# A one-core attention and gated-MLP kernel: a new order of all its operations, with other banks and other shares of work

## The chip, the cores and the metric

The kernel runs on one core of one Trainium2 chip. A core has five engines with one instruction stream each, which meet only through semaphores: PE (TensorE: matrix products into PSUM, with the weight loads as a stream of their own, PEld), DVE (VectorE), ACT (ScalarE), POOL (GpSimd) and SP (SyncE, which here only asks for transfers). Transfers are moved by 16 DMA engines; SP, ACT and POOL can ask for them. The metric is device microseconds of one execution.

## The reference, cut to what matters

Linear attention with decay, in blocks of 64 positions (4 batches, 8 heads, 768 positions, 64 channels), and on its output a gated MLP with a product over positions:

```python
for b in range(nb):                       # 12 blocks of 64
    intra = (qb @ kb.T) * Dmask           # Dmask[i,j] = lam**(i-j) for i >= j, else 0
    out[block] = intra @ vb + (qb * lam**(pos+1)) @ kv_state
    kv_state = lam**64 * kv_state + (kb * lam**(63-pos)).T @ vb
x = out, heads side by side               # 4 x 768 x 512
h = relu(x @ w_in); u, v = halves of h    # 512 each
v_n = (v - mean(v)) / sqrt(var(v) + 1e-6)
v_s = w_spatial @ v_n + b_spatial         # over the 768 positions of a batch
result = (u * v_s) @ w_out                # 4 x 768 x 512, float32
```

## The kernel before, in words

The decay is split: k is multiplied by a power of lam that falls with the position and q by its inverse, so the mask is only 0 or 1. Positions are taken in 12 steps of 256, three to a batch (step n is in batch n // 3); a step has two halves c of 128 positions.

One string, `ORDER`, names every operation in the order in which the program issues it, as `name.arguments.engine` with the engine as the last letter (T for PE, D for DVE, A for ACT, P for POOL, S for SP). A loop at the end (lines 538 to 541) calls the function for each; nothing else decides about order. Each engine runs its own operations in the order of the string; semaphores are put in where one needs another's result or a buffer or bank that is still read. The last one or two numbers of most PE operations and of their evictions are PSUM banks (0 to 6; bank 7 holds the running state).

```python
with tc.manual_schedule():
    for token in ORDER.split():
        name, *args, e = token.split(".")
        ops[name](e, *map(int, args))
```

By step n, attention:

- `LQ`, `LK`, `LV` ask for q, k, v of a step (512 KB each; line 192, SP; three buffers each). `HL.1.3` is a write of one element by POOL into the buffer that q of step 3 will use, so that this load waits for it (line 264). `GT.1.1` and `GN.2.1` are copies of one element on POOL that make it wait for the load of q of step 1 and for an operation of batch 0 (lines 239 and 464).
- `QM`, `KM` multiply halves of q and k by the decay into bfloat16 (line 289, on POOL or DVE). In steps 0 to 4 PE transposes them (`TQ`, `TK`, line 319) and ACT or DVE copies the result out (`EQ`, `EK`); from step 5 on SP asks for transposes by DMA (`DQ`, `DK`, lines 306 and 302). `VC` casts v to bfloat16 (lines 177, 179 or 181, by engine).
- `SC` makes scores (line 349), `MK` masks them on DVE (line 354), `KV` adds to the running state (line 366), `SS` copies the state out, `AV` makes the attention's output (lines 387 and 396, in two parts; `FN` is a copy of one element that stands between them), `EX` copies it out as xT.

The MLP: `PV` (line 421) and `EV` give v, `BN` its statistics, `RA`, `RD`, `RB` the reciprocal deviation and the scaled mean (lines 441, 446, 451), `VN` normalises. `RB` is needed only where ACT normalises (line 457); DVE does it from mean and deviation (line 460). `PU` (line 472) and `EU` give u. `WT` and `EW` transpose w_spatial once (line 484). For each batch `GP` copies the bias into a bank, `PW` (line 498) adds the product over positions, `GM` (line 504) multiplies with u, `PO` (line 509) is the last product, `EO` evicts and `ST` stores (line 532); the last tile goes in two halves (`PH`, `EH`, `SH`).

Constants and weights: `lam` and `BR` are asked for from ACT's queue (lines 196 and 255; 32 bytes and the bias row of 3 KB); `LB`, `LN`, `LL`, `LX` make the decay tables; `BB` spreads the bias row over all partitions by a matmul with ones (line 258, PE) and `BE` copies it out. `WI.0` asks for the half of w_in that `PV` reads, `WI.1` for the half that `PU` reads, `WS` for halves of w_spatial, `WO` for w_out: all from POOL, since they are cast on the way (lines 243, 248, 252). `tab.1` loads ACT's second table. `FL` are matmuls of ones that nobody reads (line 272).

The bias row's way, as the code has it:

```python
def b_r(e):
    {"S": nc.sync, "A": nc.scalar}[e].dma_start(out=brow, in_=moe_b_spatial.unsqueeze(0))

def b_b(e, i, b):
    nc.tensor.matmul(out=bank(b)[:, 0:HW], lhsT=one_row, rhs=brow[:, i * HW:(i + 1) * HW], start=True, stop=True)
```

Of the kernel before, what the change touches and what calls it, by code (L numbers as in the profile page):

```python
# [20 lines left out]
SC.0.1.3.4.T LK.2.S EK.1.0.0.A QM.1.1.P MK.0.0.5.6.D FL.6.256.2.0.T TQ.1.0.2.T TQ.1.1.0.T EQ.1.0.2.A EQ.1.1.0.A
LV.2.S EK.1.1.1.D VC.0.P MK.0.1.3.4.D BB.1.2.T BE.1.2.A FL.1.256.1.0.T SC.1.0.0.1.T SC.1.1.5.6.T KV.0.0.T
QM.2.1.P MK.1.0.0.1.D MK.1.1.5.6.D WI.1.P AV.0.0.2.3.T FN.0.2.3.A SS.0.0.A VC.1.A BB.0.4.T WS.0.P KV.0.1.T
AV.0.1.2.3.T BE.0.4.A TQ.2.1.0.T QM.2.0.P SS.0.1.D KM.2.1.P EX.0.1.3.A EX.0.0.2.D KV.1.0.T AV.1.0.1.6.T
# [7 lines left out]
PU.0.0.5.T EU.0.0.5.A RA.2.A PU.2.0.3.T WT.2.1.1.T EW.2.1.1.D GP.0.0.0.4.A PU.2.1.0.T EU.2.0.3.A WT.1.1.2.T
WT.0.1.6.T RD.2.D VN.2.0.D VN.2.1.D LV.4.S LQ.5.S LK.5.S EU.2.1.0.A GN.2.1.P KM.3.1.P KM.3.0.P PW.0.0.0.4.T
EW.0.1.6.D EW.1.1.2.D GP.0.2.0.5.A GP.0.3.1.3.A TQ.3.2.6.T PW.0.2.0.5.T TK.3.2.1.T GM.0.0.0.4.D EK.3.2.1.D
EQ.3.2.6.A PW.0.3.1.3.T GP.0.1.0.0.A VC.3.P KM.4.0.P GM.0.2.0.5.D SC.3.0.5.6.T SC.3.1.1.2.T GM.0.3.1.3.D
GP.0.3.0.4.A QM.4.0.P QM.4.1.P KV.3.0.T MK.3.0.5.6.D LV.5.S MK.3.1.1.2.D PW.0.3.0.4.T GM.0.3.0.4.D SS.3.0.D
# [535 lines left out]
```

## Time and profile before

| | |
|---|---|
| median of 3 runs | 144.38 us (143.93 to 144.56) |
| the profiled execution | 143.63 us, span 141.9 us |
| PE busy | 132.8 us (94%) |
| DVE, ACT, POOL busy | 110.6, 76.2, 53.5 us |
| 16 DMA engines | 31.88 MB moved, 225 GB/s on average |
| product over positions (`PW`, line 498) | 192 matmuls of 384 columns |
| granted clock of PE | 1.00 throughout |

The span is the profiler's, from the first instruction to the last; the time of the same execution is 1.73 us longer. Busy time of PE counts each matmul from its start to its modelled end, and matmuls overlap, so a busy PE may still be slower than its own pace; what counts is whether it stands idle and who let it go on. Idle time of another engine costs nothing by itself.

### The profile page before, as it was taken

How to read it: one execution, taken by the hardware profiler on the slowest of the kernel's cores; microseconds unless marked ns; L12 is line 12 of the kernel's file. 1: busy time of each engine (PE TensorE's matmuls, PEld its weight loads, DVE VectorE, ACT ScalarE, POOL GpSimd, SP SyncE). 2: the span in 40 equal slices, each digit the busy share in tenths (PEclk: the TensorE clock that was granted, in tenths of full speed). 3: DMA queues.
4: the chain of work that ended last, by engine and by line, in shares of the span. 5: the costliest groups of instructions: out<-in, count | busy, mean ns of one | idle time of the engine just before them, and what ended most of it. 6: DMA issues, size and time to landing. Idle time of an engine off the chain costs nothing.

```text
span 141.9 us, 4688 instructions
## 1 busy us (share of the span) xinstructions
PE 132.8 (94%) x1980; PEld 86.7 (61%) x1997; DVE 110.6 (78%) x220; ACT 76.2 (54%) x153; POOL 53.5 (38%) x62
## 2 busy tenths in 40 slices
PE   5979979999999999999999999999999999999990
PEld 3855656768577564676566465685665655855550
DVE  3486957998696986697899789977897989984940
ACT  3136748778527666669524647697236642570041
POOL 5567973015997532196715025603700000000000
PEclk9999999999999999999999999999999999999999
DMA  3999999999999999999999899999979242310075
GB/s 84 345 346 345 230 252 210 225 337 257 334 328 239 125 236 343 306 139 347 227 260 158 209 360 241 262 329 165 291 117 259 93 170 98 128 74 0 33 294 191
DMA packets 58232, 31.88 MB, mean 225 GB/s; under 512 B 15843, under 2 KB 55267, under 8 KB 58212
## 3 DMA queue, kind: packets, MB, share of 16 engines
q1 hardware_dynamic: 55824, 28.84, 78.1%
q0 software_dynamic: 2384, 2.75, 11.4%
q8 instruction: 15, 0.25, 0.7%
q14 instruction: 5, 0.04, 0.1%
q10 hardware_dynamic: 4, 0.00, 0.0%
HBM read 24.38 MB, written 6.29 MB: 216 GB/s over the span
## 4 chain that ended last, share of the span: by engine, by line
PE 72%; DMA 14%; DVE 4%; SPq 3%; ACT 2%; issue 1%; POOL 0%; DVEq 0%; ACTq 0%
PE ps L498 21%; PE ps L472 13%; PE ps L509 13%; PE ps L421 13%; DMA win_sb<-in_moe_w_in_dram 7%; DMA q_in<-in_q_dram 4%; DMA v_in<-in_v_dram 3%; PE ps L349 3%; PE ps L396 3%; PE ps L366 3%; DVE a_sb L354 2%; SPq L192 2%; PE ps L319 2%; PE ps L387 1%; SPq L302 1%
## 5 line engine op out<-in xcount | busy, mean ns | idle before, releaser
L498 PE MATMUL ps<-wt_sb,vn 128*128 128x384 bf16 x192 | 34.0, 326 | 0.0
L354 DVE TENSOR_TENSOR a_sb<-ps,m 128x1024 bf16<-128x1024 f32 x24 | 28.6, 1216 | 2.5 <-PE ps L349 1.9
L289 POOL TENSOR_TENSOR kc<-k_in,lv 128x512 bf16<-128x512 f32 x18 | 19.2, 1080 | 22.4 <-DMA k_in<-in_k_dram 6.3
L498 PEld LDWEIGHTS <-vn 128*128 128x128 bf16 x192 | 18.1, 98 | 12.2 <-ACT vn L457 0.4
L289 POOL TENSOR_TENSOR qc<-q_in,lqn 128x512 bf16<-128x512 f32 x19 | 20.0, 1069 | 14.2 <-DMA q_in<-in_q_dram 8.5
L472 PE MATMUL ps<-xT,win_sb 128*128 128x256 bf16 x192 | 23.2, 273 | 0.0
L421 PE MATMUL ps<-win_sb,xT 128*128 128x512 bf16 x89 | 21.8, 379 | 1.2 <-DMA win_sb<-in_moe_w_in_dram 0.6
L509 PE MATMUL ps<-wout_sb,gT 128*128 128x512 bf16 x82 | 21.1, 379 | 1.0 <-issue 0.6
L504 DVE TENSOR_TENSOR gT<-ps,uT 128x384 bf16<-128x384 f32 x32 | 16.8, 551 | 6.0 <-PE ps L498 5.3
L472 PEld LDWEIGHTS <-win_sb 128*128 128x128 bf16 x192 | 18.2, 98 | 3.6
L436 DVE BATCH_NORM_STATS2 st<-vh 128x6 f32<-128x512 bf16 x24 | 16.3, 679 | 0.8 <-ACT vh L426 0.5
L426 ACT ACTIVATE vh<-ps 128x512 bf16<-128x512 f32 x20 | 11.9, 595 | 9.3 <-PE ps L421 9.3
L177 ACT ACTIVATE o_sb<-ps 128x512 f32<-128x512 f32 (+1 forms) x17 | 9.6, 567 | 12.2 <-DVE o_sb L179 8.9
L421 PEld LDWEIGHTS <-xT 128*128 128x128 bf16 x96 | 9.1, 98 | 10.6 <-DVE xT L179 0.7
L509 PEld LDWEIGHTS <-gT 128*128 128x128 bf16 x92 | 8.5, 98 | 9.1 <-DVE gT L504 0.2
L177 ACT ACTIVATE ps<-bsp 128x384 f32<-128x384 f32 x21 | 9.9, 487 | 4.6 <-DVE a_sb L354 3.8
L177 ACT ACTIVATE xT<-ps 128x512 bf16<-128x512 f32 x16 | 9.1, 595 | 4.9 <-PE ps L396 4.9
L181 POOL CAST vb<-v_in 128x1024 bf16<-128x1024 f32 x7 | 7.8, 1118 | 8.1 <-issue 5.3
L396 PE MATMUL ps<-a_sb,vb 64*64 64x128 bf16 x384 | 10.6, 217 | 0.0
L366 PEld LDWEIGHTS <-kc 64*64 64x64 bf16 x320 | 6.8, 109 | 4.9 <-issue 3.8
L426 ACT ACTIVATE uT<-ps 128x512 bf16<-128x512 f32 x16 | 9.2, 586 | 0.4 <-PE ps L472 0.4
L366 PE MATMUL ps<-vb,kc 64*64 64x64 bf16 x320 | 8.6, 194 | 0.4 <-DVE s_sb L179 0.3
(70 smaller groups left out, 167.1 us busy)
## 6 DMA issues: line engine op xcount, KB each, us to landing
q_in<-in_q_dram SPq DMA_DIRECT2D x12, 512.0 KB, 6.6
k_in<-in_k_dram SPq DMA_DIRECT2D x12, 512.0 KB, 6.3
v_in<-in_v_dram SPq DMA_DIRECT2D x12, 512.0 KB, 6.2
out_dram<-o_sb SPq DMA_DIRECT2D x23, 256.0 KB, 2.3
wsp_raw<-in_moe_w_spatial_dram POOLq DMA_DIRECT2D x2, 576.0 KB, 10.2
win_sb<-in_moe_w_in_dram POOLq DMA_DIRECT2D x2, 512.0 KB, 8.9
wout_sb<-in_moe_w_out_dram POOLq DMA_DIRECT2D x1, 512.0 KB, 7.7
out_dram<-o_sb SPq DMA_DIRECT2D x2, 128.0 KB, 1.9
```

Source lines behind the costliest of these rows:

```text
L177: nc.scalar.activation(out=o, in_=i, func=AF.Copy)
L289: vec(e).tensor_tensor(out=dst[n % NCA][:, u].rearrange("p u m o d -> p o (u m) d"), in0=src[n % NIN].rearrange("p (o u) m d -> p o u m d" ...
L354: nc.vector.tensor_tensor(out=a_sb[n % NA][:, i].rearrange("p o w j x -> p o w (j x)"), in0=ps[:, b0:b1 + 1:b1 - b0].rearrange("p o (w y) ...
L366: nc.tensor.matmul(out=pkv[row(o), u], lhsT=kc[n % NCA][row(c), u, m, o, :], rhs=vb[n % NCA][row(c), 4 * o + u, m, :], start=new and u == ...
L396: nc.tensor.matmul(out=po[c ^ o][row(w), c, i], lhsT=vb[n % NCA][row(c), 4 * o + u, j, :], rhs=a[row(c), i, o, w, j, :], start=(r == 0 and ...
L421: nc.tensor.matmul(out=bank(b), lhsT=x[:, slot(c, g)], rhs=win_sb[:, g, DH:DFF], start=(g == 0), stop=(g == NCH - 1))
L426: nc.scalar.activation(out=o, in_=i, func=AF.Relu)
L436: nc.vector.bn_stats(out=st6[p2][:, t], in_=vh[p2][:, t])
L472: nc.tensor.matmul(out=pu[:, f2].rearrange("p (c x) -> p c x", c=2), lhsT=win_sb[:, g, f * P:(f + 1) * P], rhs=x[:, slot(0, g):slot(1, g) ...
L498: nc.tensor.matmul(out=bank(b)[:, 0:HW], lhsT=vn[bb % 2][:, s, f * P:(f + 1) * P], rhs=wt_sb[:, s, i * HW:(i + 1) * HW], start=False, stop ...
L504: nc.vector.tensor_tensor(out=gT[bb % 2][:, f, cols], in0=bank(b)[:, 0:HW], in1=uT[bb % 2][:, f, cols], op=ALU.mult)
L509: nc.tensor.matmul(out=bank(b), lhsT=gT[bb % 2][:, f, t * P:(t + 1) * P], rhs=wout_sb[:, f, :], start=(f == 0), stop=(f == NCH - 1))
```

## The change

All that differs is the string `ORDER`. It names the same operations on the same data, in another order on every engine, with other PSUM banks, and gives about a hundred of them to another engine. Line numbers stay. What differs in number: `FL` matmuls (47 in before, 44 in after) and `RB` (9 and 12: after has it for the steps 0 to 2 too, some of whose `VN` are now on ACT).

Evictions and small work by engine (before, then after):

| | ACT | DVE | POOL |
|---|---|---|---|
| `GP` bias into a bank | 21, 26 | 11, 6 | |
| `EX` xT | 16, 18 | 8, 6 | |
| `EU` u | 16, 18 | 8, 6 | |
| `EV` v | 20, 18 | 4, 6 | |
| `EQ` / `EK` transposes | 7, 4 / 4, 6 | 1, 4 / 4, 2 | |
| `SS` state | 13, 10 | 7, 10 | |
| `VN` | 10, 9 | 14, 15 | |
| `VC` cast of v | 3, 5 | 2, 1 | 7, 6 |
| `EO` / `EH` outputs | 15, 14 / 2, 0 | 8, 9 / 0, 2 | |

The requests of weights keep their places among POOL's products: `WI.0` comes behind the load of q of step 1 (in before by `GT.1.1`, in after by `QM.1.1`), `WI.1` and `WS.0` behind q's product of step 2, `WS.1` behind k's product of step 2 and beside `HL.1.3`. `BR` was the second operation of ACT and comes now behind `EK.0.0`. `BB.0`, `BB.1` stand ahead of `KV.0.0` on PE; in before `BB.1` stood ahead of `SC.1` and `BB.0` behind `AV.0.0`. The cast `VC.0` goes from POOL to ACT. On POOL a half of q's product of step 8 (`QM.8.1`) now comes ahead of those of step 7, and on SP `LK.6` comes behind the transposes of step 5.

The diff, cut to the start, the stretch with `QM.8.1`, and the end; each line is a line of the string:

```diff
--- before
+++ after
@@ ORDER @@
-msk.P one.D idn.P FL.6.256.3.1.T LQ.0.S lam.A BR.A tab.0.A row.D LK.0.S FL.2.256.2.1.T LK.1.S LB.6.T LQ.1.S
-FL.16.128.0.1.T LV.0.S LV.1.S FL.6.256.2.0.T posk.P mkc.D LN.6.A LL.D LX.A QM.0.1.D QM.0.0.P KM.0.0.P KM.0.1.D
-TQ.0.0.3.T TQ.0.1.5.T EQ.0.0.3.D TK.0.0.4.T EQ.0.1.5.A EK.0.0.4.A KM.1.0.D TK.0.1.0.T FL.4.256.1.1.T
-FL.5.256.1.0.T KM.1.1.D EK.0.1.0.D GT.1.1.P LQ.2.S WI.0.P QM.1.0.D TK.1.1.1.T SC.0.0.5.6.T TK.1.0.0.T
-SC.0.1.3.4.T LK.2.S EK.1.0.0.A QM.1.1.P MK.0.0.5.6.D FL.6.256.2.0.T TQ.1.0.2.T TQ.1.1.0.T EQ.1.0.2.A EQ.1.1.0.A
-LV.2.S EK.1.1.1.D VC.0.P MK.0.1.3.4.D BB.1.2.T BE.1.2.A FL.1.256.1.0.T SC.1.0.0.1.T SC.1.1.5.6.T KV.0.0.T
-QM.2.1.P MK.1.0.0.1.D MK.1.1.5.6.D WI.1.P AV.0.0.2.3.T FN.0.2.3.A SS.0.0.A VC.1.A BB.0.4.T WS.0.P KV.0.1.T
-AV.0.1.2.3.T BE.0.4.A TQ.2.1.0.T QM.2.0.P SS.0.1.D KM.2.1.P EX.0.1.3.A EX.0.0.2.D KV.1.0.T AV.1.0.1.6.T
-FN.1.1.6.D TQ.2.0.4.T SS.1.0.A AV.1.1.1.6.T KV.1.1.T SS.1.1.D EX.1.0.1.D eps.D EX.1.1.6.A EQ.2.1.0.A EQ.2.0.4.A
-KM.2.0.P PV.0.0.5.T EV.0.0.5.D PV.0.1.2.T EV.0.1.2.A PV.1.0.6.T BN.0.0.D BN.0.1.D TK.2.1.1.T EK.2.1.1.A
-TK.2.0.3.T EK.2.0.3.D EV.1.0.6.A PV.1.1.2.T SC.2.1.0.1.T SC.2.0.4.5.T MK.2.1.0.1.D EV.1.1.2.A tab.1.A
-MK.2.0.4.5.D RA.0.A WS.1.P HL.1.3.P LQ.3.S LK.3.S LV.3.S VC.2.P PU.1.0.3.T PU.1.1.6.T EU.1.0.3.A EU.1.1.6.A
...
-LK.8.S EX.5.0.1.D EX.5.1.6.A QM.7.1.P QM.7.0.P LV.7.S PV.5.1.6.T PV.5.0.4.T PO.0.0.5.T EV.5.1.6.A EO.0.4.2.D
-BN.4.1.D PU.5.1.6.T PU.3.1.1.T GP.1.2.1.3.D LK.9.S DQ.6.S BN.4.0.D RA.4.A BN.5.1.D EU.4.1.0.D EV.5.0.4.A
-GP.1.0.1.2.A VN.3.0.A EU.3.1.1.A EO.0.0.5.A RD.4.D RB.4.D SS.6.1.D BN.5.0.D KM.8.1.P VC.7.P DQ.7.S GP.1.2.0.5.A
-RA.5.A RD.5.D VN.4.1.D RB.5.D QM.8.0.P PU.4.0.0.T EU.4.0.0.A QM.8.1.P VN.5.1.D VN.4.0.A PO.0.1.4.T PU.5.0.1.T
...
-EO.3.2.5.D PO.3.4.2.T EO.3.4.2.A ST.3.2.S ST.3.4.S PO.3.1.3.T PO.3.3.6.T EO.3.1.3.D ST.3.1.S PH.3.5.0.3.T
-EO.3.3.6.A PH.3.5.1.5.T ST.3.3.S EH.3.5.0.3.A SH.3.5.0.S FL.1.256.0.0.T EH.3.5.1.5.A SH.3.5.1.S
+lam.A LQ.0.S posk.P row.D one.D msk.P tab.0.A LK.0.S FL.1.256.0.1.T FL.6.256.1.1.T LK.1.S idn.P LB.4.T LQ.1.S
+LN.4.A LL.D mkc.D LX.A QM.0.1.P LV.0.S QM.0.0.D FL.5.256.1.0.T FL.16.128.2.1.T KM.0.1.D LV.1.S TQ.0.1.1.T
+KM.0.0.D TK.0.1.3.T EQ.0.1.1.A TQ.0.0.5.T EK.0.1.3.A KM.1.0.P KM.1.1.D LQ.2.S TK.0.0.1.T SC.0.1.3.4.T EK.0.0.1.A
+EQ.0.0.5.D eps.D FL.8.256.0.0.T MK.0.1.3.4.D BR.A QM.1.1.P LK.2.S TK.1.1.6.T SC.0.0.1.2.T QM.1.0.D EK.1.1.6.A
+FL.3.256.5.0.T WI.0.P TQ.1.1.6.T LV.2.S TK.1.0.3.T EQ.1.1.6.D MK.0.0.1.2.D TQ.1.0.4.T EK.1.0.3.A BB.0.0.T
+EQ.1.0.4.A BE.0.0.A VC.1.P VC.0.A BB.1.2.T BE.1.2.A KV.0.0.T QM.2.1.P QM.2.0.P SS.0.0.D AV.0.0.4.5.T
+SC.1.0.0.1.T SC.1.1.2.3.T KV.0.1.T tab.1.A MK.1.1.2.3.D FL.5.256.6.0.T FN.0.4.5.A SS.0.1.A KV.1.0.T WI.1.P
+MK.1.0.0.1.D TQ.2.0.2.T AV.0.1.4.5.T WS.0.P EQ.2.0.2.A AV.1.0.3.6.T EX.0.1.5.D SS.1.0.A KV.1.1.T FN.1.3.6.D
+EX.0.0.4.D KM.2.0.P TQ.2.1.5.T AV.1.1.3.6.T SS.1.1.D KM.2.1.D EX.1.1.6.A PV.0.0.2.T EX.1.0.3.A TK.2.0.1.T
+EV.0.0.2.D PV.1.1.6.T VC.2.P EQ.2.1.5.D EK.2.0.1.D PV.0.1.3.T EV.1.1.6.A BN.0.0.D HL.1.3.P WS.1.P LQ.3.S
+SC.2.0.1.2.T TK.2.1.5.T EV.0.1.3.A LK.3.S GT.1.1.P PV.1.0.0.T EK.2.1.5.A MK.2.0.1.2.D LV.3.S SC.2.1.4.5.T
+KV.2.0.T MK.2.1.4.5.D PU.0.1.6.T AV.2.0.1.3.T BN.0.1.D PU.1.1.2.T EV.1.0.0.A LQ.4.S SS.2.0.D FN.2.1.3.A
...
+EX.5.0.0.D GN.2.1.P QM.6.1.P EU.4.1.1.A PU.4.0.2.T PV.5.0.3.T EO.0.0.5.A RA.4.A PV.5.1.4.T RD.4.D EV.5.0.3.A
+EU.4.0.2.A RB.3.D VN.3.0.D BN.5.0.D PU.5.0.0.T EV.5.1.4.A LQ.7.S DQ.6.S KM.7.0.P GP.1.1.1.1.A PU.3.1.2.T
+PU.5.1.3.T BN.5.1.D GP.1.2.1.6.A KM.7.1.P EU.5.0.0.D RA.5.A PO.0.1.4.T RD.5.D RB.4.D VN.4.1.D RB.5.D SS.6.1.A
+DK.7.S LQ.9.S VN.3.1.D VN.4.0.A EU.5.1.3.D VN.5.0.D PO.0.3.0.T VN.5.1.A EU.3.1.2.A EO.0.1.4.D LV.8.S LK.9.S
+GP.1.2.0.4.A GP.1.0.1.5.A PW.1.2.1.6.T PW.1.1.1.1.T GP.1.3.1.2.A VC.7.A QM.8.1.P QM.7.1.P QM.7.0.P PW.1.2.0.4.T
+PW.1.0.1.5.T GM.1.2.1.6.D EO.0.3.0.A GP.1.0.0.6.D GM.1.2.0.4.D GM.1.1.1.1.D DQ.7.S SC.6.1.3.4.T GM.1.0.1.5.D
...
+PO.3.1.1.T ST.3.2.S ST.3.0.S GM.3.3.1.3.D PO.3.4.3.T EO.3.1.1.D PO.3.3.4.T ST.3.1.S EO.3.4.3.A ST.3.4.S
+PH.3.5.1.1.T EO.3.3.4.A EH.3.5.1.1.D ST.3.3.S SH.3.5.1.S PH.3.5.0.5.T EH.3.5.0.5.D SH.3.5.0.S
```

More of the change, by code (lines that the diff above doesn't have):

```diff
@@ L32 @@
[L32 to L36, printed above, removed]
```

91 lines of the change are left out of this document (47 added, 44 removed).

## The prediction

> **What bounds the kernel now.** I read the page's shares first, then busy time by stage, then the chain of waits, then the start engine by engine, because only the start and the waits inside the stages can differ when the operations stay the same.
>
> ```profile
> span 141.9 us, 4688 instructions
> PE 132.8 (94%) x1980; PEld 86.7 (61%) x1997; DVE 110.6 (78%) x220; ACT 76.2 (54%) x153; POOL 53.5 (38%) x62
> q10 hardware_dynamic: 4, 0.00, 0.0%
> ```
>
> TensorE is the bound. The second answer is busy time in stages (window, its length, PE busy and then the other engines):
>
> ```profile
> 20.00:48.00 28.00, 27.40 (x428) 19.26 (x430) 23.19 (x47) 18.16 (x35) 17.01 (x19) 1.00 1.11 266
> 48.00:64.00 16.00, 15.55 (x280) 10.04 (x283) 13.02 (x30) 10.29 (x22) 6.38 (x7) 1.00 1.12 237
> 64.00:104.00 40.00, 39.63 (x562) 24.82 (x564) 33.88 (x68) 23.86 (x49) 16.59 (x16) 1.00 1.11 258
> 104.00:112.00 8.00, 7.68 (x192) 4.83 (x194) 7.15 (x10) 4.86 (x10) 0.00 (x0) 1.00 0.59 152
> 112.00:136.00 24.00, 23.84 (x202) 14.42 (x204) 20.35 (x48) 8.25 (x18) 0.00 (x0) 1.00 0.26 99
> ```
>
> From 20 to 136 us PE is idle for only 0.60 + 0.45 + 0.37 + 0.32 + 0.16 = 1.9 us. The chain of waits says what lies before that stretch (start, length, what):
>
> ```profile
> 3.26 6.18 DMA q_in<-in_q_dram
> 9.49 0.68 POOL seen L239
> 10.17 9.32 DMA win_sb<-in_moe_w_in_dram
> 19.53 0.38 PE ps L421
> ```
>
> PE's dense stretch starts at 19.53 with the first matmul of the v projection (`PV`, line 421), when the first half of `w_in` lands, and it ends at 138.33. The time is therefore the start of that stretch, plus its work, plus its waits, plus a tail of 3.6 us.
>
> The start, by ACT's and PE's own timelines:
>
> ```profile
> 1.34 0.23 ACTq L255 DMA_DIRECT2D brow<-in_moe_b_spatial_dram  x1
> 12.65 0.91 PE L258 MATMUL ps<-brow,one_row 1*128 1x384 f32 x2
> 13.60 0.49 ACT L177 ACTIVATE bsp<-ps 128x384 f32<-128x384 f32 x1 [0.33 <-PE ps L258]
> 7.93 1.45 SPq L192 DMA_DIRECT2D q_in<-in_q_dram  x1
> 16.16 0.46 ACT L177 ACTIVATE bsp<-ps 128x384 f32<-128x384 f32 x1
> ```
>
> The bias row is asked for at 1.34, 11 us before its first reader, so before hides its landing altogether.
>
> **The change, part by part.** *Work.* PE has the same matmuls in the dense stretch. Moved evictions, by their rows: ACT +5 bias copies (0.487), +2 xT (0.595), +2 uT (0.586), +2 casts of v (1.05), +2 kT (0.60), +6 small, less 2 vh, 3 qT (one full), 3 s_sb (0.38), one vn (0.81), one o_sb and the two last halves: +1.7 us. The same sum for DVE is -0.6, for POOL -1.1 (one cast of v). At 76.2 and 110.6 busy of 141.9 neither becomes the bound: I cost it at nothing. PE's matrix work hides it; if a stage lost that cover, the whole 1.7 is its price. Three `FL` matmuls fewer and the `FL` behind the last real matmul lie in idle time: nothing. Line 451 (`RB`) runs three times more, 0.207 each on DVE between reciprocal and normalisation of batch 0, beside `PU` and `PV` (8 of the projections' matmuls take 0.87 in the chain): nothing, and 0.6 if that cover is gone.
>
> *Groups of small matmuls.* Going from 128x128 to the 64x64 matmuls and back costs PE about 0.09 + 0.13 us beyond its pace, from single starts in the trace around 49.8 and 46.1. Before has 19 such groups behind the first `PV`, after has 20: +0.23.
>
> *Request of w_in.* It keeps its place behind q of step 1, but where POOL copied one element (the 0.68 above) it now does a whole half of q's product, 1.05 us by its row: issued 0.4 us later, landing at about 19.9. By itself this is +0.4. The second request goes behind two products instead of one, about 1 us later than its 15.18; its data can start only when the first request's is through, so I cost that at nothing (its reader comes four `PV`s, about 5 us, behind the dense start). `WS.1` and the hold of q now wait behind the cast of v of step 2, which waits for its load; the transposes that read `WS.1` come 13 us after the dense start, hidden; 0 to 1 us if that load is late.
>
> *Request of the bias row.* This is the largest term. `BR` goes from ACT's second place (1.34 us) to behind `EK.0.0`. That eviction waits for q's and k's products on DVE and the transposes on PE. With k of step 0 at about 6.4 us, two products (0.69 each), 8 transposes and three ACT copies of 0.60 follow: ACT is free at about 8.9. How long will the landing take? Before has one row for it: the queue that has only `lam` and this row (q10, four packets in all) moved two packets before 1.9 us and these two only then:
>
> ```profile
> core 0 of [0], span 141.9 us
> ...
> GB/s 546 410 137 751 478 137 410 410 205 273 478 273 205 410 410 205 410 410 205 410 478 0 547 478 68 478 478 137 410 478 205 273 479 341 205 274 615 205 205 683
> ...
> q10 hardware_dynamic: 2, 0.00, 2.7%
> ```
>
> That is the window 3.9 to 4.2 of the DMA answer. So 3 KB, whose issue was over at 1.57, waited until the 512 KB of q of step 0, asked for at 0.81, had gone. I read it as: a small request waits for the bytes asked for before it. At 8.9 SP stands in the middle of q of step 2 (7.93, 1.45 long). Loads land every 1.51 us (512 KB at 346 GB/s) after q of step 1 at 9.44: 10.95, 12.46, 13.97. Two thirds into the last one gives 13.5, and 13.6 with its semaphore. The lower end is the row's own time, about 2.8 us from issue: 11.7. The upper is the 6.18 of the q load in the chain: 15.1. I take 13.6, nearest to the row that shows the mechanism.
>
> The Trainium skill ("DMA: Bandwidth & Descriptors", section "Queues, rings and completion order") says otherwise: each DMA engine goes round the queues that have work, switching at packet boundaries, so that a lone row on ACT's queue would pass SP's loads. The 3.9 us above speaks against that for packets of a few descriptors and allows it if a load's whole share on an engine is one packet. By this rule the row would land near 11 and this term would be nil.
>
> PE reaches `BB.0` at about 11.6 and stands there; behind it stand `BB.1`, `KV.0.0`, `AV.0.0`, both `SC.1` and all that follows. From 13.6: `BB` 0.95 (12.65 to 13.60 above), its copy 0.49, then on ACT the cast of v of step 0, 1.05 (POOL did it in before): 16.1 for `KV.0.0`. `KV`, `AV` and `SC` took 0.65 + 0.64 in before: 17.35. Two masks on DVE, 2.35 (14.25 to 16.60 in before): 19.7. Then xT 0.68, `FN` 0.15, xT 0.68 on DVE, while PE does `AV.1.0`, `KV.1.1`, a transpose and `AV.1.1` (about 1.7): `PV` starts at 21.35 instead of 19.53, **+1.8**, and w_in is already there. The table load (1.28), moved before the state's copies on ACT, ends near 18 and hides beside the masks; with the row at 15.1 all of it moves along. The ends are +0.4 (row at 11.7, w_in is last) and +3.3.
>
> *Waits inside the dense stretch.* The new order has its own. Before's 1.9 us is the most it can win back; I find no place where evictions fall behind PE, but also none that must go better, so I take the same 1.9 (ends: -1.7 and +1.6, the latter one landing of a transpose that comes late, whose median of 4.6 us covers just the distance to its reader).
>
> *Tail.* The last two half evictions go from ACT (0.384 each) to DVE (half of 0.682): nothing.
>
> Sum on the profiled execution, 143.63 us (span 141.9 and 1.73 around it): 143.63 + 1.8 + 0.23 = 145.66. The median of the runs, 144.38, lies 0.75 above that execution, so 146.4.
>
> **The rivals.** *A: the bias row lands early.* For it: the issue itself takes 0.23 and lam, alone, moved within 0.9 us. Against it: the 3.9. Then only w_in's 0.4 and the 0.23 stay: 144.26, as a median 145.0. The Trainium skill's rule above gives this.
>
> *B: faster.* The bank handovers of the dense stretch (such as the 0.16 us that PE idles before line 509 four times) fit better in the new plan and the row is early. It needs more than 1.35 of the 1.9 us back to get below 143.66, since 0.63 is lost at the start. Taking 1.7 gives 143.3. For it: all banks are dealt anew. Against: waits of 0.1 to 0.3 each, a dozen, would have to go together by that one cause.
>
> *C: slower still, at the transposes.* POOL now has a half of q of step 8 ahead of both of step 7; it writes the buffer that step 6's transpose still reads, so step 7's transpose on SP goes out only after that lands, with three loads (1.5 each) asked for in between. If it comes after PE reaches `SC.7`, PE waits. Behind the 1.8 it would add 1 to 2.5: about 148. Against: I count some 1 to 2 us of slack there.
>
> **How the numbers follow.** Forecast 0.50 (146.4), A 0.27, B 0.09, C 0.14. The measurement tells about 0.5% (0.72 us) from no change: below 143.66 is B and a little of A (0.10); 143.66 to 145.10 is half of A and the low edge of the forecast (0.15); the rest, 0.75, is slower. The range runs from 144.2 to 148.4: the low end is A with the waits 0.8 better, the high end C or the row at 15.1 with half a microsecond more. The forecast's own range is 145.4 to 147.6.
>
> **What would show it.** The chain of waits of after should have the DMA of `brow` in it, and PE idle for about 2 us before line 258 near 11.6 to 13.6; `PV`'s first matmul near 21.4; w_in landing near 19.9 with nobody waiting; PE's idle time from there to 2 us before the tail near 1.9. If `brow` lands below 12, A is right. If PE idles before line 349 near 77 us for SP's transpose, C is. If PE idles under 0.6 us in the dense stretch, B is.

## The result, and the profile after

The changed kernel takes 149.19 us (median of 6 executions, 148.66 to 152.59), the kernel before, beside it on the same chip, 144.19 (143.37 to 145.16). The ratio is 1.034, with an interval of 1.028 to 1.040: some 5 us slower, above the range of the prediction. Executions more than 1.5% longer than the fastest of the same kernel are left out of all ratios and, unless the text says otherwise, of the medians of the experiments.

The profiled execution took 148.99 us. Its page (engines' busy time with shares, then the granted clock of PE in 40 slices):

```profile
span 147.3 us, 4677 instructions
PE 135.2 (92%) x1979; PEld 88.5 (60%) x1994; DVE 112.2 (76%) x221; ACT 78.1 (53%) x156; POOL 53.0 (36%) x61
PEclk9999599999999999999999999999999999999999
```

The span is 5.4 us longer, PE is still the bound, and there is a stretch with a granted clock of 0.5 (14.46 to 17.87 us) that the profiled execution of before did not have. Busy time by stage (window, length, PE, its weight loads, DVE, ACT, POOL, then clock, DMA share and GB/s):

```profile
24.00:48.00 24.00, 23.47 (x364) 16.43 (x368) 21.95 (x43) 16.87 (x32) 12.89 (x12) 1.00 1.02 250
48.00:64.00 16.00, 15.84 (x329) 10.02 (x321) 13.21 (x26) 8.80 (x20) 4.24 (x5) 1.00 0.86 230
64.00:80.00 16.00, 13.69 (x158) 8.74 (x158) 11.46 (x24) 9.16 (x19) 8.54 (x9) 1.00 1.18 242
80.00:104.00 24.00, 23.50 (x348) 15.09 (x352) 19.66 (x41) 15.87 (x32) 7.41 (x8) 1.00 1.13 260
104.00:112.00 8.00, 7.15 (x166) 4.80 (x165) 6.52 (x10) 1.71 (x4) 4.75 (x5) 1.00 0.47 132
112.00:136.00 24.00, 23.74 (x275) 14.70 (x277) 19.67 (x44) 12.36 (x26) 0.08 (x1) 1.00 0.39 132
```

PE's idle time from 24 to 136 us is now 0.53 + 0.16 + 2.31 + 0.50 + 0.85 + 0.26 = 4.6 us, where before it was 1.9. The pieces of the chain of waits that before's chain did not have (start, length, what):

```profile
8.28 3.92 DMA brow<-in_moe_b_spatial_dram
12.24 0.92 PE ps L258 x2
...
68.63 3.52 DMA kT<-kc
...
72.40 2.04 POOL qc L289 x2
...
74.47 5.78 DMA qT<-qc
...
97.02 5.62 DMA qT<-qc
...
103.76 1.04 POOL kc L289
104.80 0.99 POOL vb L181
```

So the end is reached through three stretches in which PE's work is not the chain: the bias row at the start (the first `PV` is at 21.05 instead of 19.53, +1.5), the transpose of q of step 7 (PE stands 2.55 us before `SC.7`, until 80.29), and the transpose of step 9, behind which POOL casts v of step 10 late (PE stands 0.69 us before `KV.10`). The last product starts 4.70 us before the end of the span, against 4.64: the tail is practically unchanged. Start 1.5, idle time 2.7 and one more group of small matmuls (0.2) make 4.4 of the 5.4; the last microsecond lies in spacings of matmuls that show no gap. Some 0.6 us of it can be placed by e2 below, whose order is the same up to there: the first 18 products over positions with the transposes among them take from 36.60 to 41.39 us in the changed kernel and from 36.11 to 40.03 in e2, 0.87 us less, of which 0.27 are idle time and counted above. In the changed kernel an operation of DVE on `vn` ends at 37.76 and one on q at 39.21, and PE goes on behind each; why they are long is the subject of the last group of experiments.

### The profile page after: what moved, and what is told of

It reads as the page before. It is cut to its first block, busy times and chain, and to the rows that moved or that the text cites. A ratio compares the mean times of both kernels' runs of the same rounds, so it can differ in the third digit from the quotient of the medians.

```text
span 147.3 us, 4677 instructions
## 1 busy us (share of the span) xinstructions
PE 135.2 (92%) x1979; PEld 88.5 (60%) x1994; DVE 112.2 (76%) x221; ACT 78.1 (53%) x156; POOL 53.0 (36%) x61
## 4 chain that ended last, share of the span: by engine, by line
PE 71%; DMA 13%; DVE 6%; POOL 3%; issue 2%; ACT 2%; POOLq 0%; SPq 0%; DVEq 0%
PE ps L421 13%; PE ps L498 13%; PE ps L509 12%; PE ps L472 11%; DMA qT<-qc 8%; PE ps L366 4%; PE ps L272 4%; PE ps L349 4%; PE ps L396 4%; DMA brow<-in_moe_b_spatial_dram 3%; PE ps L387 3%; PE ps L319 2%; DMA kT<-kc 2%; POOL qc L289 1%; DVE vn L460 1%
## 5 line engine op out<-in xcount | busy, mean ns | idle before, releaser
L289 POOL TENSOR_TENSOR qc<-q_in,lqn 128x512 bf16<-128x512 f32 x19 | 21.5, 1145 | 28.0 <-DMA qT<-qc 13.7
L421 PE MATMUL ps<-win_sb,xT 128*128 128x512 bf16 x90 | 22.7, 379 | 0.5 <-issue 0.2
L426 ACT ACTIVATE vh<-ps 128x512 bf16<-128x512 f32 x18 | 10.7, 597 | 10.7 <-PE ps L421 10.7
L177 ACT ACTIVATE ps<-bsp 128x384 f32<-128x384 f32 x26 | 12.1, 490 | 6.9 <-DVE a_sb L354 3.4
L177 ACT ACTIVATE xT<-ps 128x512 bf16<-128x512 f32 x18 | 10.1, 595 | 10.0 <-PE ps L396 10.0
L177 ACT ACTIVATE o_sb<-ps 128x512 f32<-128x512 f32 x14 | 8.2, 592 | 10.9 <-PE ps L509 10.7
L349 PE MATMUL ps<-qT,kT 64*64 64x128 bf16 x384 | 9.3, 226 | 2.7 <-DMA qT<-qc 2.5
L426 ACT ACTIVATE uT<-ps 128x512 bf16<-128x512 f32 x18 | 10.3, 586 | 1.0 <-PE ps L472 0.8
L366 PEld LDWEIGHTS <-kc 64*64 64x64 bf16 x320 | 7.8, 113 | 4.8 <-issue 3.9
```

Of the source, the lines that this page charges most:

```text
L177: nc.scalar.activation(out=o, in_=i, func=AF.Copy)
L289: vec(e).tensor_tensor(out=dst[n % NCA][:, u].rearrange("p u m o d -> p o (u m) d"), in0=src[n % NIN].rearrange("p (o u) m d -> p o u m d" ...
L366: nc.tensor.matmul(out=pkv[row(o), u], lhsT=kc[n % NCA][row(c), u, m, o, :], rhs=vb[n % NCA][row(c), 4 * o + u, m, :], start=new and u == ...
L421: nc.tensor.matmul(out=bank(b), lhsT=x[:, slot(c, g)], rhs=win_sb[:, g, DH:DFF], start=(g == 0), stop=(g == NCH - 1))
L426: nc.scalar.activation(out=o, in_=i, func=AF.Relu)
```

## The experiments

All kernels differ in tokens of `ORDER` alone. Ratios are to the kernel before, run beside each.

| kernel | edit | ratio to before (95%) |
|---|---|---|
| changed | | 1.034 (1.028 to 1.040) |
| e1 | changed, row early | 1.019 (1.009 to 1.028) |
| e4 | before, row late | 0.998 (0.993 to 1.003) |
| e5 | changed, idle matmuls at the start | 1.027 (1.020 to 1.035) |
| e2 | changed, `QM.8.1` behind step 7 | 1.028 (1.019 to 1.038) |
| e2b | e2, `DQ.7` ahead of three loads; computes something else | 1.021 (1.013 to 1.029) |
| e6 | changed, one load ahead of `DQ.5` | none: 147.13 us, and three executions of 149.69 to 151.10 |
| e6b | changed, three loads ahead of `DQ.5` | 1.007 (1.001 to 1.012) |
| e8 | before, that one load behind | 1.010 (1.006 to 1.014) |
| e9 | e1 and e6b together | 1.016 (1.012 to 1.021) |
| e10 | e9, `VC.10` early | 1.013 (1.009 to 1.016) |
| e12 | before, `QM.8.1` ahead of step 7; computes something else | none: 142.64 us, and three executions of 145.17 to 145.64 |
| e13 | e10, idle matmuls behind `BB.1` | 1.004 (0.999 to 1.008) |
| e14 | e10, POOL's step 3 as before | 1.045 (1.036 to 1.054) |
| e15 | changed, POOL's step 3 as before | 1.077 (1.070 to 1.085) |
| e16 | e14, idle matmuls behind `BB.1` | 1.058 (1.050 to 1.065) |
| e17 | before, hold of POOL taken out | 1.008 (1.003 to 1.013) |
| e18 | e14, `KM.4.0` on POOL | 1.006 (1.003 to 1.010) |
| e19 | e18, idle matmuls behind `BB.1` | 1.006 (1.001 to 1.010) |

### The start: the row, and the clock

```diff
-lam.A LQ.0.S
+lam.A BR.A LQ.0.S
...
-MK.0.1.3.4.D BR.A QM.1.1.P
+MK.0.1.3.4.D QM.1.1.P
```

> The changed kernel with the request of the bias row (BR) back at ACT's second place, nothing else moved. Theory: the late row alone costs the start of the changed kernel: there PE stands at BB.0 until 12.24 us and the cast of v behind its copy ends at 14.62, so with the row early the cast starts when v is there (about 12.3), KV.0.0 at about 13.4 instead of 14.67, the first PV at 19.8, when w_in lands, instead of 21.05, and the time falls by about 1.3, to 147.9. Rival: PE gets to SC.7 1.3 us earlier and waits as much longer there, because the transpose of step 7 stands behind loads and not behind PE's work: PV at 19.8, but the idle time before SC.7 grows from 2.5 to 3.8 and the time stays at 149.2.

Measured: 147.70 us (146.77 to 148.87), 1.5 less than the changed kernel, with the first `PV` at 20.32. By the medians the late row was worth about what the start had lost, and the first theory stands. The profiled execution of e1, the slowest of its four (148.87), is what the rival described, though: there PE waits 1.30 us at 48.97 and 2.68 before `SC.7`, which starts at 80.73 against 80.29 in the changed kernel. So in some executions the gain is waited for later, and four of them do not say how often.

The other half, the kernel before with `BR` behind `EK.0.0`:

> The kernel before with BR moved to behind EK.0.0 on ACT, the one part of the change alone. There ACT is free at about 9.2 and PE's BB.1 starts at 12.65. By the prediction's reading (a row waits for the bytes asked for before it, here q of step 2, asked for from 7.93 to 9.38 and landing near 13.9) the row lands at 13.9, BB.1 stands 1.3 us, and the time grows by 0.6 to 1.3, to 144.8 to 145.5. By what the changed kernel showed (asked for at 8.28, semaphore at 12.20, as v of step 1 landed) it lands with v, at 12.4, and nothing changes: 144.2.

Measured: 144.30 us, no change. The row, asked for at 8.42, was there at 12.34, and the matmul that reads it (timeline of PE of e4: start, length, what, idle time before it) started when ACT's eviction let it:

```profile
12.50 0.91 PE L258 MATMUL ps<-brow,one_row 1*128 1x384 f32 x2 [0.46 <-ACT qT L177]
```

So in before's order the late row costs nothing. It costs in the changed order, which puts both `BB` at 11.5 us ahead of all other work of PE. In both kernels the row landed with v of step 1, at 12.2 to 12.3, and ahead of q of step 2 (13.75 and 13.90), for which SP was asking at that moment. My 13.6 was one load too late. The row of before that I had taken it from did not show a wait for a whole load either: when it moved, at 3.9 us, at most 0.41 of the 0.52 MB of q had gone. The Trainium skill ("DMA: Bandwidth & Descriptors", "Queues, rings and completion order") has engines go round the queues at packet boundaries, which I had read as a landing near 11; the two rows lie between 11 and 13.6, at 3.9 us from the request.

For the clock:

```diff
-EK.1.0.3.A BB.0.0.T
+EK.1.0.3.A FL.6.256.0.0.T BB.0.0.T
...
-BB.1.2.T BE.1.2.A
+BB.1.2.T FL.6.256.5.0.T BE.1.2.A
```

> The changed kernel with six idle matmuls (FL) ahead of BB.0 and six behind BB.1, where PE stood 0.77 and 0.88 us; they are more work and no operation gets earlier by order. Theory: the granted clock of 0.5 from 14.46 to 17.87 us is the answer to these idle gaps; with them filled the clock stays 1.0, the scores of step 1 and the five FL behind KV.0.1 go at full pace, and PV starts 0.4 to 0.7 earlier, near 20.5; the time falls by up to 0.6, to 148.6. Rival: the halving has another cause; then the clock record looks as before and the time is the same or 0.2 longer.

Stages of the changed kernel and then of e5 (the clock is the third figure from the right):

```profile
12.00:16.00 4.00, 2.88 (x58) 2.09 (x62) 1.12 (x2) 3.17 (x5) 3.12 (x4) 0.81 1.18 305
16.00:20.00 4.00, 3.66 (x118) 2.77 (x111) 3.06 (x5) 1.72 (x5) 2.48 (x3) 0.77 1.19 246
```

```profile
12.00:16.00 4.00, 3.92 (x94) 2.52 (x91) 1.39 (x3) 3.35 (x6) 2.86 (x3) 1.00 1.18 305
16.00:20.00 4.00, 3.75 (x123) 2.82 (x119) 4.00 (x7) 1.62 (x5) 2.74 (x4) 1.00 1.21 251
```

With the gaps filled the clock stays at 1.00 and the first `PV` comes 1.1 us earlier (19.97). The time is 148.91 us, 0.3 less: not told apart from nothing. In the profiled execution PE is still about a microsecond ahead at `SC.8` (84.4 against 85.4), with a shorter wait before `SC.7` (1.54 us against 2.55), and loses it before `KV.10`, where it waits 1.64 us instead of 0.69. So what the start wins is waited for behind, which points to the middle.

### The middle: POOL's order, or the loads

The prediction's rival C laid a wait before `SC.7` to POOL, which does `QM.8.1` ahead of step 7. Undone:

```diff
-VC.7.A QM.8.1.P QM.7.1.P QM.7.0.P PW.1.2.0.4.T
+VC.7.A QM.7.1.P QM.7.0.P QM.8.1.P PW.1.2.0.4.T
```

> The changed kernel with the half of q's product of step 8 (QM.8.1) behind both of step 7 on POOL. Theory 1 (the prediction's rival C as it stands: POOL's order): QM.7.1 and QM.7.0 need no transpose to land and run at about 70.2 to 72.3; SP is free at 72.8 behind three loads, so the transpose of step 7 goes out at 72.8 instead of 74.47, lands near 78.6, and the 2.55 us before SC.7 shrink to about 0.9: 147.5. Theory 2 (the queue): the transpose lands only behind the data of the three loads asked for ahead of it, which end near 77.5 to 79.4 whenever it is asked for; then it still lands near 80 and the time stays at 149.2, less 0.3 at most.

Measured: 148.76 us, as the changed kernel within the uncertainty. Its chain of waits:

```profile
71.70 0.65 POOL qc L289
72.36 6.58 DMA qT<-qc
```

The transpose goes out 2.1 us earlier and lands only 1.3 earlier. PE still stands 2.42 us, but that is because it comes 1.2 us earlier as well, by what happened ahead of 42 us; coming as in the changed kernel it would have stood some 1.2. And the 1.3 us are lost again at once, for the granted clock is 0.5 from 79.98 to 83.40 (the 8 and the 6 in the page's line), which the changed kernel does not have there:

```profile
PEclk9999599999999999999998699999999999999999
```

So this run does not acquit POOL's order: it accounts for 1.3 us of the landing, and the time, which is no shorter, does not decide. The 6.58 us from request to landing are not POOL's: the transposes of step 5 took 3.3 and 2.7, and this one stands behind three loads asked for ahead of it. Why do they come so late? SP's timeline in the kernel before and in the changed one (start, length, what):

```profile
39.45 1.39 SPq L192 DMA_DIRECT2D k_in<-in_k_dram  x1
46.25 1.34 SPq L306 DMA_TRANSPOSE qT<-qc  x1
```

```profile
39.08 1.67 SPq L192 DMA_DIRECT2D v_in<-in_v_dram  x1
49.19 1.93 SPq L306 DMA_TRANSPOSE qT<-qc  x1
51.23 1.23 SPq L302 DMA_TRANSPOSE kT<-kc  x1
52.51 0.58 SPq L192 DMA_DIRECT2D k_in<-in_k_dram  x1
```

In the changed kernel SP stands from 40.8 to 49.19 at `DQ.5`, whose destination `AV.3` still reads, and `LK.6` with all later loads stands behind it. In before it stands there too, until 46.25, but with `LK.6` (the row at 39.45) already asked for. What the queues moved from 40 to 56 us, before and then after:

```profile
DMA packets 8220, 3.92 MB, mean 245 GB/s; under 512 B 2210, under 2 KB 8216, under 8 KB 8216
```

```profile
DMA packets 6419, 3.00 MB, mean 187 GB/s; under 512 B 2179, under 2 KB 6416, under 8 KB 6416
```

At 346 GB/s the missing 0.92 MB are 2.7 us, about the wait before `SC.7`. First one load, then all three of step 6 (`LV.6` and `LQ.6` in the same way), put ahead of `DQ.5`:

```diff
+LK.6.S DQ.5.S KM.5.1.P KM.5.0.P DK.5.S
-DQ.5.S KM.5.1.P KM.5.0.P DK.5.S
...
-EV.3.1.6.A LK.6.S GM.0.2.1.1.D
+EV.3.1.6.A GM.0.2.1.1.D
```

> The changed kernel with the load of k of step 6 (LK.6) ahead of the transposes of step 5 on SP, as it stood in the kernel before; nothing else. In the changed kernel SP stands at the transpose DQ.5 until 49.19 us with all later loads behind it; from 40 to 56 us the queues move 3.00 MB where before moved 3.92. Theory (loads shut in behind DQ.5): 0.5 MB goes into that idle time, everything behind 52 us comes up to 1.5 us (512 KB at 346 GB/s) earlier, the idle time before SC.7 falls from 2.55 to about 1.0, and the time to 147.7. Rival (POOL's order, QM.8.1 ahead of step 7): POOL's wait for the transpose of step 6 sets it, the wait at SC.7 stays within 0.5 us of 2.55, 149.2.

> The changed kernel with all three loads of step 6 (LK.6, LV.6, LQ.6) ahead of the transposes of step 5 on SP. Theory (loads shut in behind DQ.5): 1.5 MB, 4.5 us of the queue, goes into the idle time from 42 to 52, the transpose of step 7 lands before PE gets to SC.7 although POOL's order is as it was, the 2.55 us there go, and the time falls to 146.7. Rival (POOL's order): the wait at SC.7 stays above 1.5 us and the time above 148. Against both: the transposes of step 5 themselves could come later behind the loads, which would show as PE idle before SC.5 near 55.

Measured: with one load, 147.13 us in one execution and 149.69, 150.88 and 151.10 in the other three, so its time shows nothing. In the fastest, which was profiled, the timeline of PE has

```profile
78.84 0.64 PE L349 MATMUL ps<-qT,kT 64*64 64x128 bf16 x32 [1.14 <-DMA qT<-qc]
```

1.14 us where the theory said about 1.0, with PE there at the same moment as in the changed kernel (77.7). With all three, 145.62 us (median of six executions, 144.33 to 146.15): 3.5 us of the 5 are gone. The median of all ten is 146.12, still 3.1 below the changed kernel. There is no wait before `SC.7`, neither in its profiled execution (149.52) nor in that of e9 below (145.43), where the transpose of step 7 lands at 75.27 instead of 80.25. POOL's order was left as the change has it. The other direction, before with this one load behind `DK.5`:

> The kernel before with only LK.6 moved behind the transposes of step 5 on SP, the place it has after the change. Theory (loads shut in behind DQ.5): SP stands at DQ.5 until 46.25 in any case, 512 KB leave the stretch 40 to 46, and the loads and transposes behind come up to 1.5 us later. Before has the transpose of step 7 landed at 70.3, about 6 us before PE needs it, so this alone hardly shows: 0 to +0.7, 144.2 to 144.9. If it costs more than 1 us, the slack of before is smaller than I read and the place of LK.6 alone carries the loss; if nothing, the loss needs POOL's order or the late transposes of step 5 as well.

Measured: ratio 1.010, 1.4 us slower, more than the 0.7 I had allowed, and in another place. ACT's cast of v of step 6 in before and in e8, and PE in e8:

```profile
54.46 1.06 ACT L177 ACTIVATE vb<-v_in 128x1024 bf16<-128x1024 f32 x1 [1.41 <-DMA v_in<-in_v_dram]
```

```profile
55.51 1.06 ACT L177 ACTIVATE vb<-v_in 128x1024 bf16<-128x1024 f32 x1 [2.50 <-DMA v_in<-in_v_dram]
```

```profile
56.88 0.38 PE L366 MATMUL ps<-vb,kc 64*64 64x64 bf16 x13 [1.23 <-ACT s_sb L177]
```

k of step 6 lands at 53.92 instead of 45.90. POOL's product of it ends at 56.1, which alone would cost some 0.3 us, since `KV.6` starts at 55.84 in before. But v of step 6, now asked for behind it, lands at 55.42 instead of 54.37, ACT casts it and copies the state 1.05 us later, and `KV.6` on PE waits for that. PE's idle time from 48 to 64 us is 1.83 instead of 0.45 us, 1.4 more like the time. One token on SP is worth 1.0% in the faster kernel too.

Two runs did not test what they were meant to. In e2b the transpose of step 7 came ahead of the products of step 7 in the program, so it transposed what the buffer held before; in e12 `QM.8.1` overwrote a half of q of step 6 before its transpose. Both change what is computed, and the waits that the theories spoke of were not there.

> The changed kernel with QM.8.1 behind both halves of step 7 on POOL and, on SP, the transpose of q of step 7 (DQ.7) ahead of the three loads LQ.9, LV.8, LK.9. Moving QM.8.1 alone made the transpose go out 2.1 us earlier (72.36 instead of 74.47) and land only 1.3 earlier (78.98): it ran 6.58 us behind the loads' data. Theory (order of the queue): with no loads ahead it lands 3 to 4 us after its issue, near 76, before PE gets to SC.7 at 77.6; the 2.5 us there go, and the loads behind it come 2 us later; 146.7, if nothing behind needs those loads so early. Rival (the data are late in sum, whatever the order): the idle time goes from SC.7 to the readers of the loads of step 8 and 9 (before SC.8 or KV.8, near 82 to 85) and the time stays near 149.

Measured: 148.02 us; no wait before `SC.7`, but 1.80 before the scores of step 8. That the wait moves on is what the rival said of loads that are late in sum, but this run, which computes something else, does not show it.

> The kernel before with only QM.8.1 moved ahead of both halves of step 7 on POOL: the prediction's rival C by itself. There the halves of step 7 ran by 64.7, and the transpose of step 6 lands near 68, so they would run until about 71 to 72.5, the transpose of step 7 on SP goes out near 72 instead of 66.94, with DK.7 and two loads of v behind it, and lands near 75.5, DK.7's near 77, against PE at SC.7 at 76.95. Rival C as the prediction had it (POOL's order decides): 0.5 to 2 us slower, 144.9 to 146.4, with PE idle before SC.7 or a reader of the two loads of v. Rival (the loss needs the loads that were shut in behind DQ.5): the slack covers it, 144.4.

Measured: 142.64 to 145.64 us, from which nothing can be read of POOL's order, since `QM.8.1` did not wait for the transpose of step 6.

### What was left: DVE beside POOL

> The changed kernel with two parts undone: the bias row's request at ACT's second place, and the three loads of step 6 ahead of the transposes of step 5 on SP. Alone the first took 1.5 us off the median (149.2 to 147.7) and the second about 3.3 (to 145.9 in the undisturbed runs). Theory (two separate causes, one at the start, one in the queue of loads): they add up, 144.4, as fast as before within 0.6. Rival (with PE early again, it runs into the loads of the middle, and what the first wins is waited for later): 145.5 or more, and the wait of KV.10 (0.7 in the changed kernel, 2.4 in a disturbed run of the second) or one before SC.5 grows by what the start won.

Measured: 146.60 us (145.43 to 147.19), ratio 1.016: not additive, and not better than the loads alone. The rival was right in that. Then, with `VC.10.P` moved ahead of `QM.11.1.P`:

> As the run with two parts undone, and on POOL the cast of v of step 10 (VC.10) ahead of QM.11.1, which waits for the transpose of step 9 that stands on SP behind four stores. Theory: KV.10 no longer waits for POOL (0.7 us in the changed kernel), 0.5 to 0.7 less than with two, 143.8, that is 0.5 below the kernel before or level with it. Rival: the transposes of step 10 are as late, the wait moves from KV.10 to SC.10 some 6 us on, and nothing is won: as with two.

Measured: 146.34 us, 1.013: 0.3 better, less than either theory could be told by. There is no wait before `KV.10` in the trace, but there is none in e9's either, so the edit remains untested. DVE and POOL of e10 in the stretch where PE now stands:

```profile
35.61 1.05 DVE L451 SCALAR_TENSOR_TENSOR nmr<-mv,rstd 128x2 f32<-128x2 f32 x1
36.59 1.21 DVE L460 TENSOR_SCALAR vn<-vh,mv,rstd 128x512 bf16<-128x512 bf16 x1
37.72 2.32 DVE L289 TENSOR_TENSOR qc<-q_in,lqn 128x512 bf16<-128x512 f32 x1
```

```profile
35.61 2.04 POOL L289 TENSOR_TENSOR qc<-q_in,lqn 128x512 bf16<-128x512 f32 x2
37.60 0.81 POOL L252 DMA_DIRECT2D wout_sb<-in_moe_w_out_dram  x1
38.42 1.06 POOL L289 TENSOR_TENSOR kc<-k_in,lv 128x512 bf16<-128x512 f32 x1
```

These three take 0.14, 0.38 and 0.68 us at their shortest. They end 0.02, 0.15 and 0.56 us behind the end of an operation of POOL; the third stands through the request of w_out and a product. The same three in the changed kernel, and `vn` and the hold in before:

```profile
36.06 0.59 DVE L451 SCALAR_TENSOR_TENSOR nmr<-mv,rstd 128x2 f32<-128x2 f32 x1
36.57 1.19 DVE L460 TENSOR_SCALAR vn<-vh,mv,rstd 128x512 bf16<-128x512 bf16 x1
37.68 1.53 DVE L289 TENSOR_TENSOR qc<-q_in,lqn 128x512 bf16<-128x512 f32 x1
```

```profile
34.17 0.74 DVE L460 TENSOR_SCALAR vn<-vh,mv,rstd 128x512 bf16<-128x512 bf16 x2
34.97 0.18 POOL L464 CAST seen<-vn 1x1 f32<-1x1 bf16 x1 [1.65 <-DVE vn L460]
```

What DVE's operations from 24 to 48 us take beyond the shortest of their line, tile and shape (where it is over 0.15 us) adds up to nothing in before, 2.4 us in the changed kernel and 4.5 in e10. Before keeps the two engines apart: POOL stands at `GN.2.1` until `vn` is done, and POOL does `QM.3.0` and `KM.4.0`; the change gives both to DVE and moves `GN.2.1` to 60.9 us. How much is lost then depends on the moment: in the traces of e2, e1 and e13, with the same order of both engines in this stretch, the sum is 0.6, 0.9 and 1.1, in e5 3.4. The first try put `QM.3.0` and the hold back:

```diff
-EW.0.0.0.D LK.4.S QM.3.1.P RD.2.D
+EW.0.0.0.D LK.4.S QM.3.1.P QM.3.0.P RD.2.D
...
-PW.0.0.0.1.T QM.3.0.D LV.4.S KM.3.0.P
+PW.0.0.0.1.T LV.4.S GN.2.1.P KM.3.0.P
...
-EX.5.0.0.D GN.2.1.P QM.6.1.P
+EX.5.0.0.D QM.6.1.P
```

> As the run with three parts undone (146.3), and POOL's order of step 3 as in the kernel before: QM.3.0 on POOL instead of DVE, and the hold GN.2.1 ahead of KM.3.0, so that POOL's products of step 3 wait for the last vn of batch 0. Theory (POOL's products stretch DVE's small operations beside them): DVE's operations of lines 451, 460 and 289 between 30 and 40 us go back to their shortest times, the 5.0 us by which DVE's operations from 24 to 48 us exceed their shortest fall to about 0.5, the idle time of PE there (2.0) falls to 0.5, and the time to 144.8. Rival (DVE is full there by its own work, and the stretch is only waiting that shows as busy): DVE's operations get shorter but the later products of step 3 come later, PE waits for kT or scores of step 3 instead, and the time stays above 146.

> The changed kernel with only POOL's order of step 3 as before (QM.3.0 on POOL, GN.2.1 ahead of KM.3.0). Theory (POOL stretches DVE): PE's idle time between 33 and 40 us (0.43) goes and the vn and products come about 1 us earlier, but behind it the loads shut in behind DQ.5 still decide when SC.7 can go, so most of it is waited for there: 148.5 to 149.2. Rival (independent causes): a full 1.5 less, 147.7.

Both went far the other way: 150.59 us for e14, 155.53 for e15. DVE and POOL of e14:

```profile
42.56 5.77 DVE L289 TENSOR_TENSOR kc<-k_in,lv 128x512 bf16<-128x512 f32 x1
```

```profile
42.74 1.05 POOL L289 TENSOR_TENSOR kc<-k_in,lv 128x512 bf16<-128x512 f32 x1
43.74 2.04 POOL L289 TENSOR_TENSOR qc<-q_in,lqn 128x512 bf16<-128x512 f32 x2
45.74 2.03 POOL L289 TENSOR_TENSOR kc<-k_in,lv 128x512 bf16<-128x512 f32 x2
```

The half of k that DVE does (`KM.4.0`, 0.67 us alone) ends 0.56 us behind the last of five products of POOL. PE stands 4.05 us for the mask that comes behind it on DVE. The hold had moved POOL's run onto it. The theory's 144.8 fell, and the rival's "above 146" was met for a reason that it did not give: what stands is not late work of step 3 but one operation of DVE behind POOL, so the mechanism shows here more plainly than in any other run. Part of the loss is the clock: behind this stand the granted clock is 0.5 for 3.4 us in e14 and for 6.8 in e15. With that half on POOL as well:

```diff
-LV.5.S KM.4.0.D WO.P
+LV.5.S WO.P KM.4.0.P
```

> As the run with three parts undone and POOL's order of step 3 as before (150.6 in the profiled run), and KM.4.0 on POOL too, so that DVE has no product of q or k between 30 and 48 us. Theory (a product on DVE cannot go on while POOL does one): the 5.77 us of line 289 on DVE are gone, DVE's operations from 24 to 48 us exceed their shortest by less than 1.5 us, and the time is 144.5 to 145.5. Rival (POOL has too much work there): POOL's two more products, 2.1 us, make the transposes of step 5 late, PE waits before SC.4 or SC.5 between 45 and 57 us, and the time stays above 146.3.

Measured: 145.39 us (12 executions, 144.52 to 146.19), ratio 1.006. This is within the theory's range, 5.2 us below e14 and about 1 below e10; DVE's excess from 24 to 48 us is 1.5, at the edge of what the theory said. In the profiled execution PE stands 1.39 us ahead of a transpose of w_spatial at 36.16 and has no idle time from 48 to 136 us; four of its stages:

```profile
24.00:48.00 24.00, 22.61 (x336) 16.23 (x334) 19.92 (x40) 16.46 (x33) 11.91 (x13) 1.00 1.10 287
48.00:64.00 16.00, 16.00 (x345) 10.22 (x344) 13.15 (x25) 9.09 (x21) 8.15 (x9) 1.00 1.12 233
64.00:80.00 16.00, 16.00 (x225) 10.31 (x223) 13.17 (x28) 9.91 (x21) 7.77 (x8) 1.00 1.10 232
80.00:104.00 24.00, 24.00 (x347) 15.06 (x346) 20.69 (x44) 15.44 (x32) 8.86 (x10) 1.00 1.07 258
```

And the hold alone, taken out of the kernel before (`GN.2.1.P` ahead of `QM.6.0.P`):

> The kernel before with only the hold GN.2.1 moved from ahead of KM.3.1 to ahead of QM.6.0 on POOL, about where it stands after the change. Theory (POOL stretches DVE): KM.3.1 and KM.3.0 run at 33.3 to 35.3, beside the last two vn of batch 0 (34.17, 0.37 each), which then take 0.4 to 0.8 longer each; if PE waits for them, 0.4 to 1.2 us slower, 145.0 to 145.8. Rival: the vn have slack there or the products of POOL come earlier by as much: within 0.4 of 144.5.

Measured: 145.67 us, ratio 1.008, in the theory's range, and the two `vn` take 0.99 and 1.13 instead of 0.38 beside POOL's product. That PE waits for them is not shown: in the profiled execution the first `PW` comes 1.62 us later than in before (36.47 against 34.85), but the first transpose of w_spatial, ahead of those `vn`, already comes 1.63 later (29.88 against 28.25), behind a granted clock of 0.5 from 15.04 to 21.87. What makes this kernel longer stays open.

Idle matmuls at the start were also tried on e10, e14 and e18. They made no difference that holds: the medians of all executions are 146.24 against 146.34, 152.73 against 152.07, and 145.44 against 145.39. By the ratios e13 would be better, 1.004 against 1.013; but its executions fall into two groups, four from 144.08 to 144.97 us and eight from 146.07 to 147.11, and the ratio is taken from the lower six. The profiled ones show what such groups can differ in: in that of e13 (144.08) PE has no idle time from 24 to 136 us, in that of e10 (146.33) 1.99 us from 24 to 48. The clock fell to 0.5 near 14 us in the profiled execution of each all the same.

> As the run with three parts undone, and six idle matmuls behind BB.1, where PE waits for the cast of v of step 0. Theory: the granted clock stays at 1.0 (with idle time there it went to 0.5 for 3.4 us in the profiled runs of several kernels), the start is up to 0.6 us shorter, and the time is 143.3, below the kernel before by 0.6%. Rival: w_in's landing near 19.8 or the masks set the start in any case, or the halving comes only in some runs: no difference from three within 0.3.

> As the run with three parts undone and idle matmuls at the start (faster than without them in the profiled runs: 144.08), and POOL's order of step 3 as before. Theory: all four causes are out; the plan of the dense stretch is then as good as before's, and the time is 143.8 to 144.5, level with before. Rival: more than 145.3, another cause is left.

> The same with the six idle matmuls behind BB.1. Theory: as the other, less up to 0.5 for the start: 144.0 to 145.0. Rival: above 146.

No version beats the kernel before. What stays open: why the row and the loads undone together (1.016) are not better than the loads alone (1.007). The ratio of e6b rests on six of its ten executions, which may flatter it: over all of them the medians are 146.12 (e6b) and 146.87 (e9), the means 147.3 and 146.9. Of the last 0.6% of e18 the trace shows a part: its first `PV` is at 21.25, though w_in lands at 19.91, and the granted clock is 0.5 from 13.36 to 20.19. The two of its twelve executions whose mean clock was 0.997 or more took 144.61 and 144.65, as the kernel before (144.56), the other ten 145.48 in the median; two are too few to show that the clock is all of it.

## Why the prediction was wrong, step by step

**The step that failed is "Waits inside the dense stretch": "I find no place where evictions fall behind PE, but also none that must go better, so I take the same 1.9".** Idle time alone rose by 2.7 us, beyond the upper end of +1.6, and makes most of the 3.3 us between the sum (145.66) and the profiled execution (148.99). I had looked for late evictions. The waits came from transfers and from DVE beside POOL, and the edits behind them stood in front of me: `LK.6` behind the transposes of step 5 got no term at all, though SP asks in order and everything behind a standing transpose stands too (e6b, e8). Moved work was costed at nothing by sums over the whole kernel. Seven halves of q and k go from POOL to DVE and seven the other way, which such a sum cannot see, and neither they nor the move of `GN.2.1` are named in the prediction or in the table of the change. Their price depends on what POOL does at that moment (e10, e14, e18): DVE's busy time rose by 1.6 us, where the sum had said -0.6.

**Rival C** named the right place and a price near the measured one (2.55 us at `SC.7`, with "1 to 2.5" forecast), for a reason that is at most about half of it: e2 takes POOL's order back and the transpose lands 1.3 us earlier, e6b leaves that order and the wait goes. That the place was right is in part luck, since `LK.6` is not in the rival. The "1 to 2 us of slack" was read from before's transfers; in the changed kernel SP got past `DQ.5` 2.9 us later (49.19 instead of 46.25). A slack read from the old trace holds only while the transfers ahead of it keep their times.

**The start** was right in place and nearly in size: +1.5 for +1.8, and undoing it alone gave 1.5 back in the median (e1). The size was in part luck, for two terms within it were off against each other: the row landed at 12.20 and not 13.6, and of the 1.4 us that this should have saved, a half clock from 14.46 to 17.87 took most, which the prediction did not have (with the clock at 1.0, `PV` came at 19.97, e5). Rival A's landing (near 11) was not met either.

**The rest.** w_in landed at 19.78 with nobody waiting, as forecast (19.9). The tail cost nothing (0.06). The group of small matmuls (+0.23) is too small to be seen by itself. The table load, the second request of w_in and the extra `RB` did not appear in the chain as bounds of their own; the `RB` stretched to 0.6 us beside POOL are part of the loss around 36 us. Rival B was far off.

## What to carry to other kernels

When an order is planned anew, read every in-order queue that only asks for transfers: a load behind a transpose that waits for a buffer is late by the whole wait, and the loss shows far away (here 30 us later, before the scores that wait for another transpose). Price work given to DVE by what POOL does in the same microseconds, not by its own duration. A wait can be taken from one place and come back at the next, so undo suspected causes one by one and then together, and look where the idle time went.

## What the runs showed of the hardware that I had not expected

- An operation of DVE can stand through operations of POOL: 0.14 us became 1.05, 0.38 became 1.21, 0.68 became 2.32 (e10), and 0.67 became 5.77 in e14, e15 and e16, through five products of POOL in a row, all of which started after it. The Trainium skill ("SBUF — State Buffer", section "SBUF: two separate sides") says that these two engines share a pair of ports as an exclusive lock, held for a whole instruction, with which the traces agree. Which of the two goes next is not the same each time: in e14 the operation of DVE lost to five instructions of POOL, one after the other; in the changed kernel the half of q at 37.68 got in behind the first, and POOL's two products there took 2.53 us instead of 2.04.
- A row of 3 KB asked for at 8.3 to 8.6 us on a queue of its own landed 3.4 to 3.9 us later, with the load of v of step 1 and ahead of that of q of step 2 (at 12.20 in the changed kernel, 12.00 in e2, 12.34 in e4).
- The granted clock was 0.5 for 3.4 us at the start of the changed kernel after PE had stood 0.77 and 0.88 us within 3 us, and stayed at 1.00 where twelve idle matmuls filled these gaps (e5). Such gaps are not the whole condition: in e4 the clock was 0.5 from 17.81 to 21.22, with no stand of PE over 0.46 us in the 9 us before, and behind a stand of 2.42 us it fell in e2, behind one of 2.55 in the changed kernel it did not.
